# Moving v's transposes into the accumulator's PSUM tile for ten slots, one of v's copies to VectorE, and weight steps 3 to 7 up to a slot sooner

## The chip, the cores and the metric

The kernel runs on one core of a Trainium2 chip. The metric is the device time of one execution in microseconds (us), the median of several runs of the same program.

## What is computed

Attention with a sliding window, followed by a spectral mixing layer. Cut to what matters:

```python
# attention: q, k, v are [8 batches, 8 heads, 576 positions, 64]
scores = q @ k.T / sqrt(64)
rel = pos[:, None] - pos[None, :]
scores = where((rel >= 0) & (rel < 128), scores - slope[h] * abs(rel), -1e9)
x = softmax(scores) @ v                      # put together as [8, 576, 512]
# mixing: w_r, w_i are [64 modes, 512, 512] f32; w_ch is [512, 512]
X = rfft(x, axis=1)[:, :64]                  # Xr, Xi
Yr = einsum('bmd,mde->bme', Xr, w_r) - einsum('bmd,mde->bme', Xi, w_i)
Yi = einsum('bmd,mde->bme', Xr, w_i) + einsum('bmd,mde->bme', Xi, w_r)
u = x + irfft(Y, n=576, axis=1)
out = u + maximum(u @ w_ch, 0)
```

Most of the bytes are w_r and w_i, 134 MB together; q, k and v are 28 MB and the output is 9 MB.

## The kernel before

**Units, pairs and slots.** A unit is one batch and one pair of heads (128 of the 512 columns of x). Units go two by two, as pairs (two batches, same heads). There are 16 pairs: pairs 0 to 3 hold the first 128 columns of x for all eight batches (group 0), pairs 4 to 15 hold the other 384 (group 1). `_slot(g, n)` is called for n = 0 to 35 and writes out, by hand, the order of the work on every engine. Slot n works on pair d = n // 2, its first half when n is even (e = 0) and its second half when n is odd (e = 1); it prepares pair d + 1 and finishes pair d - 1. Every engine runs its own instructions in the order in which `_slot` issued them.

**What a slot does, in order.** `_score(h=0)`: the score matmuls on TensorE (L463, tile `sc`, one buffer), the exponential on ScalarE (L469), the product with the mask on VectorE (L477). In the first seven slots one more head's mask is made on ScalarE (L310). `_tr` (L413) and `_evac` (L423): a part of the next pair's q or k is transposed on TensorE into tile `tqk` (two buffers) and copied to SBUF as T; ScalarE does these copies, except four at the start. Any weight steps in the list `w0` come next. `_vnat`: v, which has been transposed once, is transposed back in 128-row pieces (L442), and VectorE copies it out (L446); this is done into the unused end of tile `av`. Then `_score(h=1)`; more `_tr`/`_evac` (in even slots two parts of q and k, in odd slots both parts of v: part 0 is 128x640, part 1 is 128x512); the casts of pair d + 2 on GpSimd (L402); one spectrum of a finished batch (L556); `_av`, the product of the probabilities with v for pair d - 1 (L494, into `av`) and its normalization on VectorE (L510, L512, and in odd slots L516); and the weight steps in the list `w1`.

**Tile `av`** has one buffer. In slot n it is written first by `_vnat` and later by `_av`; slot n + 1 may write it only when VectorE's L512 and L516 of slot n have read it. **Tile `acc`**, also one buffer, holds the weight steps' sums; it serves `_expand0` (as `xq`) and one spectrum (as `xtl`) too, all of them from slot 10 on.

**Weight steps of group 0.** `_quad(g, u)`, u = 0 to 31, multiplies four modes of w_r (u even) or w_i (u odd) with the spectra (L756, 16 matmuls). Steps 4c to 4c + 3 add up in one `acc` tile, which ScalarE copies out after the last of them (`_evac0`, L768). `_expand0` spreads the spectra of eight modes (xq L736 on TensorE, L737 and L741 on VectorE into `z0`); it runs in the slot whose `w1` begins with a step divisible by 4. The main loop hands each slot its steps: slots 10 and 11 in the call of `_slot` in the second loop, slots 12 to 31 by the tuple `share`.

**Loads.** All loads are issued by SyncE in one program order and run on the same 16 DMA engines. q, k and v of a pair are six loads of 288 KB (L375). A weight step's load is 1 MB (L654). Steps 0, 1, 4 and 5 are loaded into a ring of four places, 2 and 3 into a spare place; from step 6 on, a load of step u goes to place u % 4, whose content must have been used. `_send` runs after each slot from slot 10 on and issues the loads that the counter `g.used` allows:

```python
need = u - 3 if u >= 8 else u - 5      # group 0
if g.used < need:
    return
```

After slot 35 come the weight steps of group 1, `_pair` (L790), whose loads of 1.5 MB (L671) go through a ring of three places in the same manner; in this stage TensorE does the other half of the mixing (L837, L841, L842) beside them. `_finish` then adds up and stores the output (L824, L960, L963).

Of the kernel before, what the change touches and what calls it, by code (L numbers as in the profile page):

```python
# [9 lines left out]
FP32 = mybir.dt.float32  # L10
# [6 lines left out]
P = 128  # L17
# [16 lines left out]
def kernel(  # L34
# [16 lines left out]
    g = Ctx()  # L51
# [57 lines left out]
    with tc.manual_schedule(engines={ET.SP, ET.PE, ET.Activation, ET.DVE, ET.Pool}):  # L109
        with ExitStack() as wctx:  # L110
            wpool = wctx.enter_context(tc.tile_pool(name="wpool", bufs=1))
            A = len(GROUPS[-1])
            g.wring = wpool.tile([P, RING * 2 * A * DM], FP32)
            aux = g.wring[:, 4 * QUAD * DM :].bitcast(BF16)
            g.sel = aux[:, 0 : QUAD * P].rearrange("p (a c) -> p a c", a=QUAD)
            g.z0 = aux[:, 512:1280].rearrange("p (a i m b) -> p a i m b", a=QUAD, i=3, m=MB)
            g.own = aux[:, 1280:1344]
            g.own4 = g.wring[:, 4 * QUAD * DM + 700 : 4 * QUAD * DM + 704]
            g.used = 0
            mctx = ExitStack()  # L120
            g.mpsum = mctx.enter_context(
                tc.tile_pool(name="mpsum", bufs=1, space=bass.MemoryType.PSUM, side="right"))
            with ExitStack() as actx:
                g.work = actx.enter_context(tc.tile_pool(name="work", bufs=2))
                g.ps2 = actx.enter_context(
                    tc.tile_pool(name="ps2", bufs=1, space=bass.MemoryType.PSUM))
                g.ps1 = actx.enter_context(
                    tc.tile_pool(name="ps1", bufs=2, space=bass.MemoryType.PSUM))

                loaded = (g.first[1] + LA) // 2  # L130
                first = [(d, w) for d in range(loaded) for w in range(3)]
                first[3 * loaded - 3 : 3 * loaded - 3] = [(None, 1), (None, 4)]
                first[3 * loaded - 6 : 3 * loaded - 6] = [(None, 0)]
                first.append((None, 5))
                _begin(g, first)
                n1 = H - 1
                with tc.tile_pool(name="tmpc", bufs=1, side="right") as tp:
                    _consts(g, tp)
                    for w in range(3):
                        _cast(g, 0, w)  # L140
                    _consts2(g)
                    for w in range(2):
                        for part in range(2):
                            _tr(g, 0, w, part)
                            _evac(g, 0, w, part, nc.vector if w == 1 else None)
                    for w in range(2):
                        _cast(g, 1, w)
                    nc.scalar.activation(g.one, g.one, AF.Exp, scale=-1.0)
                    _mask(g, 0)
                    for n in range(n1):  # L150
                        _begin(g, first)
                        _slot(g, n)
                        if n == 3:
                            _select(g)
                    _begin(g, first)
                    assert not first
                start = g.first[1] + 2
                zx = ctx.enter_context(tc.tile_pool(name="zx", bufs=1, side="right"))
                g.ZTa = zx.tile([P, 4, 4, 2, 16, 8], FP32)
                spare = g.ZTa.rearrange("p e k i m b -> p (e k i m b)").rearrange("p (w r) -> p w r", w=2)  # L160
                for u in (2, 3):
                    _load_q(g, u, spare[:, u % 2])
                g.sent = 6
                for n in range(n1, start + 2):
                    if g.first[1] <= n <= start and n % 2 == 0:
                        _load(g, n // 2 + LA // 2)
                        if n == start:
                            _load(g, n // 2 + LA // 2 + 1, (0, 1))
                    _slot(g, n, [2] if n > start else [], [[0, 1], [3]][n - start] if n >= start else [])
                    if n >= start:  # L170
                        _send(g)

                share = ((), (4,)), ((5,), (6,)), ((7,), (8,)), ((), (9,)), ((10,), (11,)), ((), (12,)), \
                    ((), (13,)), ((), (14,)), ((), (15,)), ((), (16,)), ((), (17,)), ((), (18,)), \
                    ((), (19,)), ((), (20, 21)), ((22,), (23,)), ((), (24, 25)), ((26,), (27,)), \
                    ((), (28, 29)), ((), (30,)), ((), (31,))
                for n in range(start + 2, N + 2 + TAIL):
                    if n % 2 == 0:
                        _load(g, n // 2 + LA // 2, (2,))
                        _load(g, n // 2 + LA // 2 + 1, (0, 1))  # L180
                    i = n - start - 2
                    _slot(g, n, *(share[i] if i < len(share) else ()))
                    _send(g)
                    if N - 7 <= n < N - 3:
                        _load_wch(g, n - N + 7)
                    if N - 2 <= n < N + 2:
                        _cast_wch(g, n - N + 2)
            zp = ctx.enter_context(tc.tile_pool(name="zpool", bufs=1, side="right"))
            g.ZT = g.ZTa.bitcast(BF16).rearrange("p e k a m (b t) -> p e k (a m) b t", t=2)[..., 0]
            g.Z = zp.tile([P, B, DM], BF16)  # L190
            g.ZW = zp.tile([P, B, DM], BF16)
            last = len(GROUPS) - 1
            with ExitStack() as xctx:
                xt = xctx.enter_context(tc.tile_pool(name="xts", bufs=2))
                xps = xctx.enter_context(
                    tc.tile_pool(name="xps", bufs=2, space=bass.MemoryType.PSUM))
                eps = xctx.enter_context(
                    tc.tile_pool(name="eps", bufs=1, space=bass.MemoryType.PSUM))
                ftq = _ft_steps(g, xt, xps)
                g.Xz = {}  # L200
                _expand(g, 0, xt, xps)
                k, xT = 0, None
                for i in range(NM - 4):
                    m, w = divmod(i, 2)
                    m *= 2
                    _pair(g, m, w)
                    _send(g)
                    if i % MB == 5:
                        _expand(g, m // MB + 1, xt, xps)
                    if i == 2 * RING - 1:  # L210
                        xT = _xt(g, 0, xt, xps)
                    while k < len(g.seq) and k * (NM - 4 - 2 * RING) < (i + 1 - 2 * RING) * len(g.seq):
                        nxt = _xt(g, k + 1, xt, xps) if k + 1 < len(g.seq) else None
                        _xw(g, k, xT, xps)
                        xT, k = nxt, k + 1
                    if i > 2 * RING and ftq:
                        ftq.pop(0)()
                    if 0 <= i - (NM - 14) < B:
                        _z_early(g, i - (NM - 14), eps)
            g.fps = ctx.enter_context(  # L220
                tc.tile_pool(name="fps", bufs=3, space=bass.MemoryType.PSUM))
            g.mm, g.y = {}, {}
            for i in range(3):
                _known(g, i)

            wps = mctx.enter_context(
                tc.tile_pool(name="wps", bufs=1, space=bass.MemoryType.PSUM))
            g.idle = wps.tile([P, DM], FP32)
            for m in (NM - 4, NM - 2):
                for w in range(2):  # L230
                    _pair(g, m, w, BUSY)
                    _send(g)
            mctx.close()
        _finish(g)
# [73 lines left out]
def _mask(g, h):  # L308

    g.nc.scalar.activation(g.mask[:, h], g.rel, AF.Exp, scale=-(2.0 ** (-8.0 * (h + 1) / g.H)))  # L310
# [122 lines left out]
def _vnat(g, d, e, av):  # L433
# [2 lines left out]
    u = g.two[d]  # L436
    i0, n = ((0, 3), (6, 2))[e]
    c0 = (4 + e) * (g.D + 1) + e
    vt = av[:, :, c0 : c0 + n * g.D].bitcast(BF16)
    for i in range(2 * n):  # L440
        h, t = divmod(i0 + i, g.ST)
# [152 lines left out]
def _slot(g, n, w0=(), w1=()):  # L594
# [3 lines left out]
    d, e = divmod(n, 2)  # L598
# [20 lines left out]
    av = g.ps2.tile([P, 2, 512], FP32, tag="av", name="av") if here or old else None  # L619
    if here:  # L620
        _vnat(g, d, e, av)
        _score(g, d, e, 1)
# [6 lines left out]
    if e == 1 and nxt:  # L629
        for part in range(2):  # L630
            _tr(g, d + 1, 2, part)
            _evac(g, d + 1, 2, part)
    if d + 2 < N:
        for w in ((0,), (1, 2))[e]:
            _cast(g, d + 2, w)
# [361 lines left out]
```

## Time and profile before

| | before |
|---|---|
| median of 3 runs | 436.73 us (436.57 to 437.23) |
| the profiled execution's own time | 438.21 us |
| its span in the profile | 436.4 us |
| TensorE / VectorE / ScalarE / GpSimd busy | 73% / 53% / 49% / 24% |
| q, k, v and weights, read from HBM | 163.58 MB |
| mean DMA rate over the span | 398 GB/s |

The span runs from the first to the last instruction on the core. Busy shares are averages over stages with different limits: slots 0 to 35 take the first 168 us, the weight steps of group 1 follow up to about 400 us, `_finish` takes the rest. ScalarE's two exponentials per slot (L469) tell where the slots lie: slot 4 begins at 30.77 us, slot 8 at 48.44, slot 10 at 56.90, slot 11 at 63.33, slot 12 at 67.87, slot 17 at 92.92. "Granted clock" is the share of TensorE's full clock that the profile records. A wait is told as who waited and what ended the wait.

### The profile page before, as it was taken

To read this page: it belongs to the slowest core of one execution; us is meant where nothing else is said; L and a number is where in the kernel's file an instruction comes from. 1 tells how busy PE (TensorE), PEld (TensorE's weight loads), DVE (VectorE), ACT (ScalarE), POOL (GpSimd) and SP (SyncE) were. 2 spreads that over 40 slices of the span, in tenths; PEclk is the share of its full clock that TensorE was granted. 3 is DMA by queue.
4 is the path that set the end of the run, shared out by engine and by line. 5 is a ranking of instruction groups with operands and counts; after the bars stand their busy time and mean duration, and the time that the engine had idled before them with its cause. 6 is when DMAs were issued, how large, how long until landed. Compare 5 with 4: busy or idle time off the path is not lost.

```text
span 436.4 us, 11040 instructions
## 1 busy us (share of the span) xinstructions
PE 316.5 (73%) x4684; PEld 206.1 (47%) x4684; DVE 230.6 (53%) x420; ACT 215.1 (49%) x326; POOL 103.0 (24%) x160
## 2 busy tenths in 40 slices
PE   2778798878889787556766655756656588879994
PEld 1456566666667664433343333333333355535552
DVE  6466877757787674053243243332532454612884
ACT  4799978778898660122243222222222234312883
POOL 8755545433454201000000000000000000000983
PEclk9988999989999997586578688666686778969999
DMA  8999999999999999999999999999999999993787
GB/s 298 409 412 417 416 362 382 372 417 421 418 419 381 421 429 430 426 426 430 428 416 430 426 419 425 430 430 427 429 430 426 430 427 418 413 425 140 281 316 273
DMA packets 33665, 173.73 MB, mean 398 GB/s; under 512 B 3792, under 2 KB 3792, under 8 KB 21456
## 3 DMA queue, kind: packets, MB, share of 16 engines
q1 hardware_dynamic: 33616, 173.03, 96.8%
q8 instruction: 36, 0.59, 0.5%
q14 instruction: 13, 0.11, 0.1%
HBM read 163.58 MB, written 9.44 MB: 396 GB/s over the span
## 4 chain that ended last, share of the span: by engine, by line
DMA 44%; PE 26%; ACT 15%; DVE 11%; issue 3%; SPq 0%; POOL 0%; ACTq 0%; POOLq 0%
DMA wring<-in_moe_w_r_dram 23%; DMA wring<-in_moe_w_i_dram 21%; ACT att L469 7%; PE acc L790 4%; DVE att L477 3%; ACT T L423 3%; PE sc L463 2%; PE acc L756 2%; PE mm L824 2%; PE av L494 2%; PE y L824 2%; PE tqk L413 2%; DVE x_sb L512 2%; PE xw L837 2%; PE av L442 1%
## 5 line engine op out<-in xcount | busy, mean ns | idle before, releaser
L841 ACT CAST hl<-xw 64x512 bf16<-64x512 f32 x72 | 41.8, 580 | 119.6 <-PE xw L837 85.1
L790 PE MATMUL acc<-Xz,wring 128*128 128x32 bf16 x1464 | 48.8, 183 | 63.8 <-DMA wring<-in_moe_w_i_dram 35.3
L790 PEld LDWEIGHTS <-wring 128*128 128x128 bf16 x1464 | 43.4, 101 | 95.4 <-DMA wring<-in_moe_w_i_dram 50.3
L842 DVE TENSOR_TENSOR hl<-xw,hl 64x512 bf16<-64x512 f32 x72 | 49.6, 689 | 66.2 <-ACT hl L841 64.1
L963 POOL TENSOR_TENSOR o<-r,ys 128x512 f32<-128x512 f32 x18 | 22.6, 1278 | 230.9 <-DVE r L955 229.5
L469 ACT ACTIVATE att<-sc 128x1024 bf16<-128x1024 f32 x64 | 67.0, 1047 | 19.6 <-PE sc L463 19.3
L477 DVE TENSOR_TENSOR att<-att,hl 128x1024 bf16<-128x1024 bf16 x64 | 54.9, 857 | 38.8 <-ACT att L469 38.4
L423 ACT COPY T<-tqk 128x640 bf16<-128x640 bf16 x92 | 66.1, 770 | 4.5 <-PE tqk L413 4.4
L402 POOL CAST hl<-hl 128x576 bf16<-128x576 f32 x64 | 44.4, 722 | 50.2 <-issue 36.9
L837 PE MATMUL xw<-wch,xT 128*128 128x512 bf16 x144 | 53.1, 507 | 1.0 <-ACT FT L350 1.0
L413 PE MATMUL tqk<-ident_b,hl 128*128 128x128 bf16 x288 | 27.8, 237 | 9.7 <-POOL hl L402 6.4
L463 PE MATMUL sc<-T,T 64*128 64x256 bf16 (+2 forms) x320 | 26.5, 261 | 6.5 <-ACT att L469 5.2
L817 DVE COPY xT<-tp 128x512 bf16<-128x512 bf16 x36 | 15.1, 421 | 29.9 <-PE tp L815 29.6
L402 POOL CAST b<-hl 128x576 bf16<-128x576 f32 x32 | 25.3, 816 | 17.1 <-issue 10.8
L413 PEld LDWEIGHTS <-hl 128*128 128x128 bf16 x288 | 19.3, 105 | 18.9 <-issue 8.4
L837 PEld LDWEIGHTS <-xT 128*128 128x128 bf16 x144 | 17.2, 125 | 20.9 <-issue 15.7
L494 PE MATMUL av<-hl,att 128*128 128x65 bf16 (+1 forms) x576 | 24.0, 199 | 3.3 <-DVE hl L446 1.9
L587 ACT CAST Xz<-xz 128x384 bf16<-128x384 f32 x16 | 7.7, 479 | 34.8 <-PE xz L581 24.7
L442 PE MATMUL av<-ident_b,T 128*128 128x128 bf16 x160 | 15.2, 229 | 11.1 <-DVE x_sb L512 6.6
L494 PEld LDWEIGHTS <-att 128*128 128x128 bf16 (+1 forms) x576 | 20.3, 102 | 6.3 <-issue 2.3
L512 DVE TENSOR_TENSOR x_sb<-av,rec 128x512 bf16<-128x512 f32 x32 | 22.1, 691 | 1.1
L756 PE MATMUL acc<-wring 128*128 128x64 bf16 x480 | 18.7, 193 | 4.5 <-DMA wring<-in_moe_w_i_dram 1.6
(112 smaller groups left out, 454.7 us busy)
## 6 DMA issues: line engine op xcount, KB each, us to landing
wring<-in_moe_w_i_dram SPq DMA_DIRECT2D x30, 1536.0 KB, 10.1
wring<-in_moe_w_r_dram SPq DMA_DIRECT2D x30, 1536.0 KB, 10.1
wring<-in_moe_w_r_dram SPq DMA_DIRECT2D x15, 1024.0 KB, 9.1
wring<-in_moe_w_i_dram SPq DMA_DIRECT2D x15, 1024.0 KB, 9.2
hl<-in_q_dram SPq DMA_DIRECT2D x32, 288.0 KB, 6.6
hl<-in_k_dram SPq DMA_DIRECT2D x32, 288.0 KB, 6.2
hl<-in_v_dram SPq DMA_DIRECT2D x32, 288.0 KB, 7.7
out_dram<-o SPq DMA_DIRECT2D x32, 256.0 KB, 2.9
```

Of the source, the lines that this page charges most:

```text
L402: g.nc.gpsimd.tensor_copy(u.b[w][:, :, e], u.raw[w][e])
L413: g.nc.tensor.transpose(u.tp[:, r - r0], u.b[w][:, r].rearrange("p u d -> p (u d)"), g.ident_b)
L423: copy(u.T[w].rearrange("c h (p r) -> c (h p) r", r=g.R)[:, :, r0:r1], u.tp[:, 0 : r1 - r0].rearrange("c r p -> c p r"))
L463: nc.tensor.matmul(sc[:, e, c0 : c0 + nq], lhsT=kT[es, h, _start(kt) : _start(kt) + P], rhs=qT[es, h, kt * P : kt * P + nq], start=True, s ...
L469: nc.scalar.activation(a, sc, AF.Exp, scale=1.0 / math.sqrt(g.D))
L477: nc.vector.tensor_tensor(out=a, in0=a, in1=m, op=ALU.mult)
L494: nc.tensor.matmul(av[o, h, t * (D + 1) : (t + 1) * (D + 1)], lhsT=u.att[min(kt // 2, 1), h][:, f, c0 : c0 + m], rhs=vn[:, g.ST * h + kt, ...
L512: nc.vector.tensor_tensor(out=xo, in0=avv[:, :, 0:4, 0:D], in1=rec[:, :, 0:4].unsqueeze(-1).broadcast_to([P, 2, 4, D]), op=ALU.mult)
L790: nc.tensor.matmul(acc[:, et, :, m - c0 : m - c0 + 2, :], lhsT=w[:, a].bitcast(BF16)[:, 1::2][:, et * P : (et + 1) * P], rhs=X[:, a, 1 - k ...
L837: nc.tensor.matmul(xw, lhsT=xT[:, dt], rhs=g.wch[:, dt], start=(dt == 0 and g.way[n] != "q"), stop=(dt == 3))
L841: nc.scalar.copy(g.hl[hi, n, h], xw[hi])
L842: nc.vector.tensor_tensor(out=g.hl[lo, n, h], in0=xw[hi], in1=g.hl[hi, n, h], op=ALU.subtract)
```

## The change

In slots 0 to 9, `_vnat` transposes into a fresh `acc` tile (named `vt`) instead of the end of `av`. In the odd ones of these slots the copy of v's second part (128x512) goes to VectorE instead of ScalarE. Five weight steps run up to a slot sooner: 3 goes from the end of slot 11 to its middle, and 4 from the end of slot 12 to the end of slot 11; with it goes the `_expand0` of steps 4 to 7. 5 and 6 go from slot 13 to slot 12, and 7 from the middle of slot 14 to the end of slot 13. From step 8 on all is as before. `_send` is not edited, but sees `g.used` grow sooner: the load of step 8 is issued after slot 11 instead of slot 12, those of 9 and 10 after slot 12 instead of 13, that of 11 after slot 13 instead of 14. SyncE's order of loads changes accordingly. No work is added or dropped.

```diff
-                    _slot(g, n, [2] if n > start else [], [[0, 1], [3]][n - start] if n >= start else [])
+                    _slot(g, n, [2, 3] if n > start else [], [[0, 1], [4]][n - start] if n >= start else [])
...
-                share = ((), (4,)), ((5,), (6,)), ((7,), (8,)), ((), (9,)), ((10,), (11,)), ((), (12,)), \
+                share = ((5,), (6,)), ((), (7,)), ((), (8,)), ((), (9,)), ((10,), (11,)), ((), (12,)), \
...
     c0 = (4 + e) * (g.D + 1) + e
+    if 2 * d + e < g.first[1] + 2:
+        av, c0 = g.mpsum.tile([P, 2, 256], FP32, tag="acc", name="vt"), 0
     vt = av[:, :, c0 : c0 + n * g.D].bitcast(BF16)
...
         for part in range(2):
             _tr(g, d + 1, 2, part)
-            _evac(g, d + 1, 2, part)
+            _evac(g, d + 1, 2, part, g.nc.vector if part and n < g.first[1] + 2 else None)
```

Here `start` is 10 and `g.first[1]` is 8.

## The prediction

> **What bounds the kernel now.** I read the page first: the chain that ended last, and the slices of the span for DMA.
>
> ```profile
> DMA 44%; PE 26%; ACT 15%; DVE 11%; issue 3%; SPq 0%; POOL 0%; ACTq 0%; POOLq 0%
> ...
> GB/s 298 409 412 417 416 362 382 372 417 421 418 419 381 421 429 430 426 426 430 428 416 430 426 419 425 430 430 427 429 430 426 430 427 418 413 425 140 281 316 273
> ```
>
> Loads set the end: up to slice 36 the DMA engines deliver 410 to 430 GB/s, except in slices 5 to 7 and 12. The bytes do not change, so the loads end sooner only where such a hole closes; `_finish` follows them at its own pace. Table by stretch (length, busy time of PE, PEld, DVE, ACT, POOL, clock, DMA share, GB/s):
>
> ```profile
> 17.00:57.00 40.00, 31.08 (x443) 22.50 (x441) 28.15 (x51) 38.22 (x55) 23.02 (x34) 0.91 1.03 414
> ...
> 62.00:66.00 4.00, 3.36 (x75) 2.80 (x72) 2.69 (x6) 2.72 (x5) 1.95 (x4) 1.00 0.79 285
> 66.00:74.00 8.00, 6.91 (x132) 5.37 (x133) 5.80 (x12) 6.75 (x10) 3.69 (x6) 1.00 1.04 403
> 74.00:82.00 8.00, 6.45 (x127) 5.07 (x127) 6.16 (x11) 7.00 (x10) 3.47 (x5) 1.00 0.95 334
> 82.00:134.00 52.00, 44.16 (x768) 33.74 (x765) 39.24 (x70) 44.06 (x59) 23.16 (x35) 0.97 1.02 417
> 134.00:138.00 4.00, 4.00 (x84) 3.21 (x85) 2.54 (x6) 2.65 (x5) 0.66 (x2) 1.00 0.89 336
> ```
>
> Time lost against the neighbours' rate: first hole (412 - 285) x 4 / 412 = 1.2 us, second (417 - 334) x 8 / 417 = 1.6, third (421 - 336) x 4 / 421 = 0.8. SyncE's timeline shows why (start, duration, line, load):
>
> ```profile
> 57.92 1.03 SPq L375 DMA_DIRECT2D hl<-in_k_dram  x2
> 62.37 0.56 SPq L654 DMA_DIRECT2D wring<-in_moe_w_r_dram  x1
> ...
> 72.50 0.55 SPq L654 DMA_DIRECT2D wring<-in_moe_w_r_dram  x1
> ```
>
> SyncE is silent from 58.95 to 62.37: the load of step 6 waits for step 0, the end of slot 10. The k load issued at 58.63 took 5.8 us to land, so the engines ran dry at 64.4. It waits again until 72.50 with the load of step 8, which needs step 4's place (slot 12). Both are releases by TensorE in the slots' order, so the question is how much sooner these come.
>
> **What bounds slots 1 to 9.** In 17 to 57 us ScalarE is busy 38.22 of 40 us: it sets the pace there, at about 4.15 us a slot. Its gaps come from TensorE, and TensorE's from VectorE's reading of `av` (idle before an instruction in brackets):
>
> ```profile
> 50.01 0.49 PE L442 MATMUL av<-ident_b,T 128*128 128x128 bf16 x6 [1.26 <-DVE x L516]
> ...
> 50.87 1.02 ACT L469 ACTIVATE att<-sc 128x1024 bf16<-128x1024 f32 x1 [0.73 <-PE sc L463]
> ```
>
> **Part 1, `vt` in its own tile.** In slots 2 to 9 `_vnat` no longer waits for L512/L516 of the slot before. `acc` is unused until slot 10, and its only earlier reader is L446 of the slot before, long done. Of the waits removed only two reach ScalarE: 0.87 us before slot 5's first exponential (36.38) and the 0.73 above. Gain: up to 1.6 us. `_av` still waits for L512/L516, but a few matmuls later.
>
> **Part 2, the copy on VectorE.** Five 128x512 copies (slots 1, 3, 5, 7, 9) leave ScalarE. Two copies, 640 and 512 wide, start at 47.23 and the next exponential at 48.44, 1.21 us later, so one of 512 is worth about 0.58; five are 2.9 us, all where ScalarE is the bound. On VectorE the same form cost 710 ns (L423, 128x512, two instances at the start): 5 x 0.71 = 3.6 us. VectorE has 11.9 us idle in 17 to 57, but the copy lies in a chain: exponential, product (0.85), copy (0.71), `_vnat` (0.5), scores (0.4), next slot's second exponential. Walking slots 1 to 9 with these durations, the exponentials come 0.2 us sooner in slot 2, 0.8 in slot 4, 1.5 in slot 6 and 2.6 in slot 8; not more, because this chain replaces ScalarE's queue as the limit. From slot 7 VectorE itself is full: from the first product of slot 7 (45.85) to L516 of slot 9 (57.73) it works 11.9 us with 1.8 idle, and gets two more copies of 0.63 net of overlap. It starts that stretch 1.5 us sooner and ends it 1.7 sooner. Slot 10's spectra, transposes and steps 0 and 1 hang on that L516. So the end of slot 10 comes **1.7 us sooner** (bounds: 4.5, all of both parts, and -1.3, if nothing but VectorE's two extra copies counted).
>
> [...]
>
> **Part 3, the weight steps.** Their number and cost are unchanged: 16 matmuls in 0.63 us. Slot 11 now holds steps 2, 3 and 4, `_expand0` (L736 1.03 on TensorE, L737 0.69 and L741 0.58 on VectorE) and `_evac0` (0.59 on ScalarE), which `xq` must wait for, since both use `acc`. Behind that wait TensorE queues v's transposes and `_av`. With the durations of slot 12 I get step 4's end 1.2 us after step 3's old end (67.35), that is at 68.5 instead of 72.46, and slot 12 starting 1.1 us later. Slots 12 to 14 get it back: slot 12 loses the expansion (4.96 becomes 4.4, as slot 13 took), 13 and 14 have one step less each, and 14 is then like the old 12 (4.96 instead of 5.44). By slot 15 the sum is +0.1. In the data nothing is short: loads of 2 to 5 landed by 53 us.
>
> Now the loads. Step 6's goes out at 62.37 - 1.7 = 60.7, before the engines run dry at 64.4: the first hole closes. Steps 6 and 7 keep them busy until 64.4 + 2 x 2.45 = 69.3 (1 MB at 420 GB/s takes 2.45-2.5). Step 8's load goes at 68.5 - 1.7 = 66.8 instead of 72.50, with v, q and k directly behind it on SyncE; those of 9 and 10 at about 71 instead of 73.6 and 76.9. The second hole closes too. q and k of pair 11 land about when they did (their casts come 20 us later). Closed: 1.2 + 1.6 = 2.8 us; since packets run slower while few are queued, I keep 0.2 of loss.
>
> Does compute use it? In slot 16 TensorE stood still for a load:
>
> ```profile
> 91.76 0.64 PE L756 MATMUL acc<-wring 128*128 128x64 bf16 x16 [1.61 <-DMA wring<-in_moe_w_i_dram]
> 92.33 0.40 PE L463 MATMUL sc<-T,T 64*128 64x256 bf16 x6
> ...
> 94.00 0.42 PE L463 MATMUL sc<-T,T 64*128 64x256 bf16 x6 [0.72 <-ACT att L469]
> 94.36 1.03 PE L736 MATMUL xq<-hl,wring 128*128 128x128 bf16 x4
> 95.21 1.14 PE L413 MATMUL tqk<-ident_b,b 128*128 128x128 bf16 x9
> ```
>
> That load (step 11) is now issued a slot sooner and this wait goes. Slot 17 then starts 1.7 + 1.6 - 0.1 = 3.2 us sooner, and the slots keep that. The loads are 2.6 ahead, compute 3.2; the third hole, which is SyncE waiting for step 20 while the engines drain, shrinks by the difference, 0.6 at most; I count 0.5. From 180 us on loads run without a hole (426 GB/s), so the lead reaches `_finish` whole.
>
> Sum: 1.2 + 1.6 - 0.2 + 0.5 = **3.1 us**. Against the profiled execution that is 438.21 - 3.1 = 435.1, its span 433.3; that execution lies 1.5 us above the median, so the median becomes 436.73 - 3.1 = **433.6 us**.
>
> **Rivals.** A difference under 0.2% (0.9 us) cannot be told from none here.
>
> *A, the forecast*: 55%, 432.4 to 434.8.
>
> *B, TensorE's clock.* In the lines above, `tqk` x9 takes 1.14 us where it took 0.68 in slot 15: from 94 to 98 us the granted clock is 0.56, after a stretch (90.8 to 94.2) in which TensorE was busy 1.72 of 3.4 us because of the 1.61 wait. Without the wait the spell may go, and with it 0.5 + 0.5 + 0.3 us of slow matmuls and the 1.64 us for which ScalarE then waited (99.02), partly the same. Compute gains 1.1 more, and the third hole closes fully: 0.3 to 1 us on top of the forecast, 432.2. The same spells at 22.6 to 26 and 32.8 to 36.2 follow stretches with 2.0 of 3.4 us busy and may go or move. 13%. [...]
>
> *C, no gain before slot 10.* If VectorE's chain gives back all that ScalarE saves, the first hole stays, step 8's load still goes 4 us sooner, the second hole closes and the 1.6 us wait goes: 1.5 us, 435.2. For it: VectorE's full stretch from slot 7. Against it: two gaps of ScalarE vanish in any case. 15%.
>
> *D, nothing measurable*: the packets stay slow in 74 to 82 (the DMA share is 0.95 there, at only 334 GB/s) though the loads come sooner, and C holds. 5%, 436.5.
>
> *E, slower: v's copy blocks TensorE.* It lies behind the product on VectorE, and `_vnat` of the next slot, with scores, transposes and `_av` queued behind it on TensorE, waits for it. If every one of the five copies lengthened its slot by 0.71 and ScalarE's 0.58 went into waiting, slot 10 would end 3.6 us later, the first hole would be 4.8 us, the second would close: 3.6 - 1.6 = 2.0 slower, 438.7. It decides from a delay of slot 10 of over 1.6 us. Against it: in even slots the removed waits for L512/L516 (0.66 to 1.26 us) are longer than the delay. 12%.
>
> **How the numbers follow.** The forecast is A's. Eight in ten: from B's better end, 431.8, to beyond C, 436.2; D and E and a little of the rest lie outside. Faster by over 0.2%: A, B, and most of C, 80%; within 0.2%: D and C's edge, 8%; slower: E, 12%.
>
> **What would show it.** Right: in the changed profile step 0 ends near 60.6 us, the load of step 8 is issued near 67, slices 5 to 7 read over 400 GB/s, no wait for a load stands before step 11, five L423 copies of 0.71 us appear on VectorE, and L442 waits for T there instead of L516. Wrong: slot 10 ends at 62 us or later, or these slices stay below 390, or a hole of the same size opens later.

## The result: 0.5% faster, and where the time came from

The changed kernel took 435.22 us (median of 22 runs, 434.65 to 438.8); the kernel before, run beside it, 437.67 us (22 runs, 435.96 to 439.48). The ratio of their means is 0.9951, with a 95% interval of 0.9936 to 0.9966: about 2.1 us faster (1.5 to 2.8; the medians lie 2.45 us apart). The two profiled executions lie further apart: 434.88 us with a span of 433.1, against 438.21 and 436.4, that is 3.3 us.

The page of the changed kernel, chain that ended last and DMA rate in 40 slices:

```profile
DMA 58%; PE 22%; ACT 10%; DVE 6%; issue 2%; SPq 0%; ACTq 0%
...
GB/s 289 409 412 414 418 413 396 416 421 415 418 418 422 424 432 426 395 423 433 428 423 434 426 423 431 431 424 432 417 429 432 424 426 426 426 415 128 285 315 275
```

Counted from 0, slices 5 to 7, which read 362, 382 and 372 before, now read 413, 396 and 416, and slice 12 went from 381 to 422. Slice 16 fell from 426 to 395. The table by stretch (length, busy time of PE, PEld, DVE, ACT, POOL, granted clock, DMA share, GB/s):

```profile
17.00:57.00 40.00, 32.36 (x464) 23.86 (x461) 32.36 (x61) 37.17 (x51) 25.15 (x34) 0.91 1.03 413
62.00:66.00 4.00, 3.58 (x74) 2.90 (x71) 3.16 (x6) 3.49 (x6) 1.89 (x4) 1.00 1.05 432
66.00:74.00 8.00, 6.89 (x145) 5.38 (x141) 6.37 (x11) 7.47 (x11) 4.19 (x7) 1.00 1.00 386
74.00:82.00 8.00, 6.51 (x103) 4.67 (x100) 5.93 (x12) 6.95 (x10) 3.40 (x5) 1.00 1.03 426
82.00:134.00 52.00, 45.32 (x820) 34.53 (x819) 40.54 (x74) 45.35 (x61) 23.23 (x34) 1.00 1.02 418
134.00:138.00 4.00, 2.33 (x39) 1.78 (x40) 1.61 (x3) 2.70 (x5) 1.78 (x3) 1.00 1.00 418
```

All three holes are closed (285, 334 and 336 before; 432, 426 and 418 now), and the clock is full from 82 to 134 us. Of these stretches only 66 to 74 reads lower than before: (412 - 386) x 8 / 412 = 0.5 us lost there. But a new hole opens behind them, in slice 16 (before, then now):

```profile
174.00:182.00 8.00, 4.44 (x123) 3.56 (x121) 0.72 (x2) 0.96 (x2) 1.44 (x10) 0.50 1.01 426
```

```profile
174.00:182.00 8.00, 4.48 (x124) 3.65 (x121) 0.00 (x0) 0.26 (x1) 0.00 (x0) 0.50 0.96 383
```

That is (426 - 383) x 8 / 426 = 0.8 us. When the same kernel was profiled again (the first run below), it read 423 GB/s there, so this hole belongs to the one execution. SyncE's timeline shows the releases (start, duration, line, load; the line numbers behind `_vnat` are two higher than before):

```profile
58.06 1.05 SPq L375 DMA_DIRECT2D hl<-in_k_dram  x2
60.28 0.56 SPq L656 DMA_DIRECT2D wring<-in_moe_w_r_dram  x1
60.93 0.55 SPq L656 DMA_DIRECT2D wring<-in_moe_w_i_dram  x1
66.29 0.54 SPq L656 DMA_DIRECT2D wring<-in_moe_w_r_dram  x1
```

Step 6's load leaves at 60.28 instead of 62.37, step 8's at 66.29 instead of 72.50. And step 11 in TensorE's timeline starts 4.64 us sooner, with no wait in brackets:

```profile
87.12 0.63 PE L758 MATMUL acc<-wring 128*128 128x64 bf16 x16
```

In the chain of waits the last weight load ends at 398.47 before (start and duration, one line of each kernel):

```profile
388.86 9.61 DMA wring<-in_moe_w_i_dram
```

and at 395.18 now:

```profile
385.62 9.56 DMA wring<-in_moe_w_i_dram
```

3.3 us sooner, which is the whole difference of the spans. In the experiments' profiles too the span ended 37.8 to 38.1 us after the last weight load had landed, so the end follows this landing.

### The profile page after: what moved, and what is told of

It is laid out like the page before. It is cut to its first block, busy times and chain, and to the rows that moved or that the text cites. A ratio compares the mean times of both kernels' runs of the same rounds, so it can differ in the third digit from the quotient of the medians.

```text
span 433.1 us, 11017 instructions
## 1 busy us (share of the span) xinstructions
PE 317.3 (73%) x4684; PEld 206.2 (48%) x4684; DVE 232.8 (54%) x425; ACT 212.4 (49%) x321; POOL 104.3 (24%) x160
## 4 chain that ended last, share of the span: by engine, by line
DMA 58%; PE 22%; ACT 10%; DVE 6%; issue 2%; SPq 0%; ACTq 0%
DMA wring<-in_moe_w_r_dram 30%; DMA wring<-in_moe_w_i_dram 19%; PE acc L792 4%; ACT att L471 4%; DMA hl<-in_k_dram 3%; DMA hl<-in_q_dram 3%; PE mm L826 2%; DMA ZTa<-in_moe_w_r_dram 2%; PE av L496 2%; PE acc L758 2%; PE y L826 2%; PE xw L839 2%; ACT T L423 2%; DVE att L479 2%; DVE hl L844 1%
## 5 line engine op out<-in xcount | busy, mean ns | idle before, releaser
L792 PEld LDWEIGHTS <-wring 128*128 128x128 bf16 x1464 | 43.3, 101 | 94.8 <-DMA wring<-in_moe_w_i_dram 51.3
L423 ACT COPY T<-tqk 128x512 bf16<-128x512 bf16 (+1 forms) x87 | 62.2, 758 | 4.2 <-PE tqk L413 3.6
L402 POOL CAST hl<-hl 128x576 bf16<-128x576 f32 x64 | 46.1, 748 | 45.2 <-issue 33.4
L839 PE MATMUL xw<-wch,xT 128*128 128x512 bf16 x144 | 55.2, 524 | 0.7 <-ACT FT L350 0.7
L758 PEld LDWEIGHTS <-wring 128*128 128x128 bf16 x480 | 16.3, 99 | 6.0 <-DMA wring<-in_moe_w_r_dram 2.6
```

Of the source, the lines that this page charges most:

```text
L402: g.nc.gpsimd.tensor_copy(u.b[w][:, :, e], u.raw[w][e])
L423: copy(u.T[w].rearrange("c h (p r) -> c (h p) r", r=g.R)[:, :, r0:r1], u.tp[:, 0 : r1 - r0].rearrange("c r p -> c p r"))
L758: nc.tensor.matmul(acc[:, et, :, h : h + QUAD, :], lhsT=w[:, a].bitcast(BF16)[:, 1::2][:, et * P : (et + 1) * P], rhs=g.z0[:, a, 1 - k : 3 ...
L792: nc.tensor.matmul(acc[:, et, :, m - c0 : m - c0 + 2, :], lhsT=w[:, a].bitcast(BF16)[:, 1::2][:, et * P : (et + 1) * P], rhs=X[:, a, 1 - k ...
L839: nc.tensor.matmul(xw, lhsT=xT[:, dt], rhs=g.wch[:, dt], start=(dt == 0 and g.way[n] != "q"), stop=(dt == 3))
```

## The experiments

Part 1 is `vt` in the `acc` tile, part 2 the five copies of v on VectorE, part 3 the weight steps (with the sooner loads that follow from them). Diffs are against the changed kernel, except the last, which is against the kernel with the old lists of steps. Ratios are against the kernel before, with 95% intervals; the other columns come from one profiled execution each.

| kernel | median us (runs) | ratio | span us | step 0 starts | step 8's load |
|---|---|---|---|---|---|
| whole change, run again | 435.68 (6) | 0.9939 (0.9922 to 0.9956) | 433.6 | 59.32 | |
| parts 1 and 2 | 436.75 (12) | 0.9973 (0.9954 to 0.9991) | 435.0 | 59.02 | 69.80 |
| parts 1 and 2, again | 436.03 (12) | 0.9968 (0.9949 to 0.9987) | 433.6 | 59.82 | |
| part 3 alone | 436.17 (12) | 0.9960 (0.9944 to 0.9977) | 434.4 | 60.69 | 67.37 |
| all, loads of 8 to 11 held back | 435.34 (6) | 0.9932 (0.9915 to 0.9950) | 433.1 | 59.60 | 68.05 |
| part 1 alone | 435.86 (5) | 0.9955 (0.9933 to 0.9977) | 433.4 | 59.20 | 69.98 |
| part 1 alone, again | 435.85 (12) | 0.9966 (0.9949 to 0.9984) | 433.4 | 59.48 | |
| part 2 alone | 440.24 (6) | 1.0052 (1.0025 to 1.0080) | 439.1 | 64.70 | |
| parts 1 and 3 | 435.31 (12) | 0.9942 (0.9924 to 0.9960) | 433.6 | 59.48 | |
| parts 1 and 2, step 11 a slot later | 436.19 (8) | 0.9954 (0.9938 to 0.9970) | 433.4 | 59.60 | |
| before, step 11 a slot later | 437.11 (12) | 0.9990 (0.9970 to 1.0011) | 435.4 | 61.25 | |
| before, second profile | 437.98 (1) | | 436.2 | 60.70 | |

**The whole change once more**, no edit:

> The whole change again, as the yardstick for the kernels run beside it. Both theories: ratio 0.995 (0.9935 to 0.9965), about 2.1 us faster; step 0 starts near 59.6 us, no hole over 0.3 us in the loads between 58 and 66 us and 0.5 us lost between 66 and 72 us.

435.68 us, ratio 0.9939. It repeats, and serves as the mark for the kernels run beside it.

**Parts 1 and 2 without part 3**: the old lists of steps.

```
-  _slot(g, n, [2, 3] if n > start else [], [[0, 1], [4]][n - start] if n >= start else [])
+  _slot(g, n, [2] if n > start else [], [[0, 1], [3]][n - start] if n >= start else [])
...
-  share = ((5,), (6,)), ((), (7,)), ((), (8,)), ((), (9,)), ((10,), (11,)), ((), (12,)), \
+  share = ((), (4,)), ((5,), (6,)), ((7,), (8,)), ((), (9,)), ((10,), (11,)), ((), (12,)), \
```

> Parts 1 and 2 alone (v's transposes in their own tile for ten slots, five copies on VectorE); the weight steps stay where they were. Theory (an earlier end of slot 10 moves every later load, so it closes both holes): step 0 starts near 59.6 us, step 6's load goes at 60.3, step 8's at 70.4 instead of 72.5, while the engines stay busy to 73.7; the second hole shrinks from 1.6 to 0.5 us and step 11's wait of 1.6 us mostly goes; 2.3 us faster or nearly what the whole change gives. Rival (each part closes one hole, the gains add): only the first hole closes, 1.2 us faster, and 74 to 82 us stays near 334 GB/s.

Its table by stretch, columns as above:

```profile
62.00:66.00 4.00, 3.33 (x66) 2.60 (x63) 3.15 (x6) 3.76 (x6) 2.06 (x3) 1.00 1.05 421
66.00:74.00 8.00, 6.51 (x130) 5.24 (x129) 6.52 (x12) 6.94 (x10) 4.60 (x6) 1.00 1.03 402
74.00:82.00 8.00, 6.59 (x113) 4.94 (x110) 5.59 (x10) 6.46 (x9) 2.73 (x5) 1.00 1.00 408
82.00:134.00 52.00, 44.24 (x762) 33.94 (x760) 38.18 (x70) 42.22 (x56) 22.45 (x32) 0.93 1.01 412
134.00:138.00 4.00, 4.00 (x84) 3.28 (x83) 2.52 (x6) 3.85 (x6) 1.62 (x2) 1.00 0.84 303
```

Both early holes all but closed without part 3, and yet the gain was 1.2 us (0.27%). The last but one line and the last tell why in this execution: at step 11 TensorE waited longer than before,

```profile
89.80 0.64 PE L758 MATMUL acc<-wring 128*128 128x64 bf16 x16 [2.35 <-DMA wring<-in_moe_w_i_dram]
```

then ran at half clock from 90.3 to 97.2, and step 20 came at 132.66, only 1.26 us sooner than before (133.92). So the third hole grew to (421 - 303) x 4 / 421 = 1.1 us. The loads were ahead, the slots not.

**Part 3 alone**: parts 1 and 2 taken out.

```
-    if 2 * d + e < g.first[1] + 2:
-        av, c0 = g.mpsum.tile([P, 2, 256], FP32, tag="acc", name="vt"), 0
...
-            _evac(g, d + 1, 2, part, g.nc.vector if part and n < g.first[1] + 2 else None)
+            _evac(g, d + 1, 2, part)
```

> Part 3 alone (weight steps 3 to 7 sooner, and their loads with them); slots 0 to 9 as before. Theory: step 0 starts at 61.7 us as before, the first hole stays (62 to 66 us near 285 GB/s), step 8's load goes near 68.5 us, the second hole closes (74 to 82 us over 415 GB/s), step 11 does not wait: 1.5 us faster. Rival (without the earlier slots the crowded slot 11 costs what the loads gain): no difference, slot 12 and all after it 1 us later.

```profile
62.00:66.00 4.00, 3.62 (x71) 2.91 (x68) 2.24 (x5) 3.18 (x5) 1.28 (x2) 1.00 0.95 370
66.00:74.00 8.00, 6.84 (x141) 5.36 (x138) 6.49 (x13) 7.47 (x10) 4.09 (x7) 1.00 0.94 363
74.00:82.00 8.00, 6.60 (x116) 4.89 (x117) 5.75 (x12) 6.95 (x11) 3.90 (x6) 1.00 1.03 426
...
134.00:138.00 4.00, 2.17 (x45) 1.70 (x42) 1.91 (x4) 2.99 (x5) 2.42 (x4) 1.00 1.00 421
```

Nearly the mirror image: the first hole does not close but spreads (370 GB/s in 62 to 66 us, (412 - 370) x 4 / 412 = 0.4 us lost, and 363 in 66 to 74, another 1.0), the second and third close, step 11 (88.21) has no wait and step 20 comes at 129.45. 1.7 us (0.40%), near the 1.5 that rival C had for this.

**Do the sooner loads do it, or the sooner steps?** The whole change, with the loads of steps 8 to 11 held back by a slot or so:

```
-            need = u - 3 if u >= 8 else u - 5
+            need = {8: 6, 9: 8, 10: 8, 11: 9}.get(u, u - 3) if u >= 8 else u - 5
```

> The whole change, but the loads of steps 8 to 11 are held back to the slots after which they went before the change (needs of 6, 8, 8 and 9 used steps instead of 5, 6, 7 and 8), so SyncE's order of loads is that of before. Theory (part 3 acts through the loads): step 8's load goes near 70 us instead of 66.3, as in the kernel with parts 1 and 2 alone, and the time is that kernel's, 0.3 to 0.8 us slower than the whole change. Rival (part 3 acts through TensorE's order, the loads were early enough): same as the whole change within 0.2 us.

No change in time (0.9932 beside 0.9939), although step 8's load left 1.76 us later than in the whole change (not the 3.7 expected):

```profile
68.05 0.55 SPq L656 DMA_DIRECT2D wring<-in_moe_w_r_dram  x1
```

Step 11, at 88.05, waited 0.77 us for its load, and no spell of slow clock followed. 66 to 74 us reads 412 GB/s here instead of 386, so the 0.5 us lost there was not decisive either. My theory fell: the loads were soon enough without their sooner release. That part 3 works through the place of the steps in TensorE's order is what is left, but it is not shown. TensorE came to step 11 at 87.28 us here (88.05 - 0.77) and at 87.45 with parts 1 and 2 alone (89.80 - 2.35), almost the same; the waits differ because the load landed 1.75 us sooner here.

**Part 1 alone**, the old lists of steps (as above) and:

```
-            _evac(g, d + 1, 2, part, g.nc.vector if part and n < g.first[1] + 2 else None)
+            _evac(g, d + 1, 2, part)
```

> Part 1 alone: v's transposes in their own tile in slots 0 to 9; no copy moves, the weight steps stay. Walk of the prediction: only the two gaps of ScalarE that end with scores queued behind a wait for L516 go (0.87 and 0.73 us), step 0 starts 0.7 to 1.6 us sooner (60.1 to 61.0 us). Rival (the waits are only moved to the product with v at the slot's end): 61.5 to 61.8 us. The time follows the compute lead at step 20: 0 to 1 us faster.

0.9955, and run again 0.9966. That is already most of the gain. ScalarE's load is unrelieved (busy 39.29 of 40 us from 17 to 57 us, 37.17 in the whole change), but step 0 comes no later. The profiles of all kernels here, grouped by what they do in slots 0 to 9, say why (starts in us; the normalization is the last of slot 9 on VectorE, on which slot 10 hangs, L516, in the changed kernels L518):

| slots 0 to 9 | normalization | slot 10 on ScalarE | step 0 |
|---|---|---|---|
| as before (4 profiles) | 56.42 to 57.45 | 55.88 to 56.90 | 60.69 to 61.71 |
| part 1, without the copies (3) | 54.94 to 55.22 | 54.39 to 54.67 | 59.20 to 59.48 |
| parts 1 and 2 (6) | 54.75 to 55.50 | 53.56 to 54.31 | 59.02 to 59.82 |

With the copies ScalarE begins slot 10 about 0.5 us sooner, but VectorE's normalization and step 0 come no sooner than without them. Part 1 alone brings all of it: 1.7 us, by the means behind the first two rows.

**Part 2 alone**: the old lists of steps (as above), and `vt` back in `av`.

```
-    if 2 * d + e < g.first[1] + 2:
-        av, c0 = g.mpsum.tile([P, 2, 256], FP32, tag="acc", name="vt"), 0
```

> Part 2 alone: the five copies of v on VectorE; v's transposes stay in the tile of the product, and wait for L516 of the slot before, which now comes 0.6 us later in odd slots. If part 2 needs part 1: step 0 starts at 61.2 us or later, less than 0.5 us sooner, and the waits of L442 for L516 grow to 1.5 to 2 us. Rival (ScalarE's saving counts by itself): step 0 starts near 60 us.

0.5% slower. In TensorE's timeline (idle before the instruction in brackets):

```profile
32.59 0.79 PE L442 MATMUL av<-ident_b,T 128*128 128x128 bf16 x6 [1.81 <-DVE x L516]
...
42.41 0.51 PE L442 MATMUL av<-ident_b,T 128*128 128x128 bf16 x6 [1.18 <-DVE x L516]
...
51.40 0.51 PE L442 MATMUL av<-ident_b,T 128*128 128x128 bf16 x6 [1.78 <-DVE x L516]
```

The copies delay L516, and with `vt` still in `av` every second `_vnat` stands behind it, for 1.81, 1.18 and 1.78 us where before it stood for 1.26, 0.66 and 1.26. A half-clock spell (53.1 to 60.0) follows the last of them, step 0 comes at 64.70, 3 us later than in the first profile of before, and 62 to 66 us falls to 233 GB/s. How much of this is the waits' and how much the spell's is not separated. This is close to rival E, made real by taking away part 1; only that `_vnat` waits here for L516, which the copies delay, and not for the copy itself.

**Parts 1 and 3, without part 2**: the `_evac` edit of part 1 alone, on the new lists.

> Parts 1 and 3, without the copies on VectorE. If part 2 is worth nothing once part 1 is there (step 0 started at 59.2 us with part 1 alone and at 59.0 with parts 1 and 2): step 0 starts at 59.2 us, the time is that of the whole change within 0.2%, ratio 0.994 to 0.995. Rival (part 2 pays where ScalarE is the bound): step 0 a microsecond later than in the whole change, near 60.5, and 0.3% slower than it.

0.9942 beside the whole change's 0.9939. Part 2 brings nothing that can be measured here. This is the simpler version and not a faster one.

**Part 1 alone again, and parts 1 and 2 again**, to weigh part 2 once more with more runs:

> Part 1 alone, a second time, beside parts 1 and 2 on the same chip. Theory (the times differ by whether TensorE's clock halves after the wait for step 11): the profile shows no half clock between 85 and 100 us and the ratio is 0.995 to 0.996 again, or it shows one and the ratio is near 0.997. Rival (part 2 costs by itself): 0.2% faster than parts 1 and 2 whatever the clock does.

> Parts 1 and 2 alone, a second time. Theory: ratio near 0.997 together with a half clock after the wait for step 11 near 90 us and under 330 GB/s in 134 to 138 us; without that spell the profiled execution is 1.5 us shorter in its span than the first one (435.0), like part 1 alone. Rival: the same span near 435 us with no such spell.

0.9966 and 0.9968: no difference. Part 1 alone, which was expected at 0.995 to 0.996 without a half clock at step 11, came out a little above that: there was none there (a wait of 0.92 us, clock 1.00 from 86 to 98 us), but one at 128.4 to 131.8. The second profile of parts 1 and 2 has a shorter wait and no slow clock near 90 us (one at 58.1 to 61.5 instead):

```profile
89.68 0.64 PE L758 MATMUL acc<-wring 128*128 128x64 bf16 x16 [0.82 <-DMA wring<-in_moe_w_i_dram]
```

```profile
134.00:138.00 4.00, 2.95 (x58) 2.40 (x57) 2.21 (x6) 3.74 (x6) 2.61 (x4) 1.00 1.01 412
```

Its third hole is almost gone and its span is 433.6 instead of 435.0. So the same kernel with and without the spell behind step 11 differs by 1.4 us, one execution each, though step 0 was 0.8 us later in the faster one and its three stretches from 62 to 82 us read lower (393, 386 and 384 GB/s).

**Is it step 11's wait?** Parts 1 and 2 with step 11 a slot later (it goes from the end of slot 16 to the middle of slot 17, and step 10 from the middle of slot 16 to its end):

```
-  share = ((), (4,)), ((5,), (6,)), ((7,), (8,)), ((), (9,)), ((10,), (11,)), ((), (12,)), \
+  share = ((), (4,)), ((5,), (6,)), ((7,), (8,)), ((), (9,)), ((), (10,)), ((11,), (12,)), \
```

> Parts 1 and 2, and of part 3 nothing; instead step 11 goes from the middle of the pair at the end of slot 16 to the middle of slot 17, so that TensorE reaches it after its load has landed (89.8 us in the kernel with parts 1 and 2 alone, where it waited 2.35 us and the clock was halved for 6.8 us). Theory (the gain is the smaller of the loads' lead and the slots' lead at step 20, and the wait with the half clock behind it took the slots' lead): no wait for a load at step 11, no half clock between 85 and 100 us, step 20 starts at 130.5 us or sooner, 134 to 138 us over 400 GB/s, ratio 0.994 to 0.995 like the whole change. Rival (steps 3 to 7 themselves had to come sooner): like parts 1 and 2 alone, ratio 0.997.

0.9954. Step 11 at 89.57 waits 0.42 us, no slow clock follows, step 20 comes at 129.56 (132.66 without the edit), and the third hole is gone:

```profile
134.00:138.00 4.00, 2.46 (x44) 1.80 (x41) 2.11 (x4) 3.24 (x6) 2.29 (x3) 1.00 1.00 420
```

The span is 433.4, as in the whole change, with steps 3 to 10 not moved sooner at all. In the times the step is within the intervals (0.9973 and 0.9968 without the edit), so this rests on the profile.

**The same single move in the kernel before** (the edit just shown, without parts 1 and 2), and the kernel before profiled again:

> The kernel before with one step moved: 11 goes from slot 16 to the middle of slot 17, nothing else. Theory (the time is set by the loads' holes; the slots' lead at step 20 decides the third): holes one and two stay, TensorE does not stand still at step 11 and keeps its clock, step 20 starts 1.5 us or more sooner than 133.9 us, 134 to 138 us goes from 336 to over 400 GB/s, 0.8 us faster. Rival (the third hole follows from the first two, whose lost time moves the loads): no difference.

> The kernel before, once more, for its profile. If the half clock follows the wait for step 11 by chance of where the clock's windows fall: a spell of another length (none, 3.4 or 6.8 us) starting between 88 and 98 us, and the longer it is, the lower the rate in 134 to 138 us and the longer the span. Rival: the same spell of 3.4 us from 94 us and 336 GB/s in 134 to 138 us.

The move alone gives 0.9990, with an interval (0.9970 to 1.0011) that holds both no change and the 0.8 us expected: not resolved. Its profile shows the mechanism: no stand before step 11, and

```profile
134.00:138.00 4.00, 3.03 (x62) 2.38 (x60) 2.67 (x5) 2.64 (x4) 1.74 (x2) 1.00 1.02 421
```

with a span of 435.4 beside 436.4 and 436.2. The second profile of before has the wait again (1.89 us) and again 3.4 us of slow clock behind it (93.3 to 96.7), and 317 GB/s in the third hole. Its spells of slow clock in the early slots lie elsewhere (one at 21.6 to 28.5, none at 32.8 to 36.2). Its step 0 starts at 60.70, a microsecond sooner than in the first profile (61.71), and its first hole is small (399 GB/s).

## Why the prediction was right, and which of its terms were not

**Direction and range held, and the mechanism in the main.** The holes that were to close did, by the releases that were named. Step 0 ended at 60.25 us (forecast 60.6), step 8's load left at 66.29 (66.8), slot 12 began at 66.62 (67.3), the first two holes closed, step 11's wait went, and its last named sign held too: `_vnat` waits for T now and no longer for L516 (TensorE's timeline of the changed kernel):

```profile
31.81 0.51 PE L444 MATMUL vt<-ident_b,T 128*128 128x128 bf16 x6 [0.77 <-DVE T L423]
```

For the profiled pair the sum was 3.1 and the span shrank by 3.3, but that they meet so closely is partly luck. Two of the terms were off in opposite directions: 0.5 instead of 0.2 was lost between 66 and 74 us, and the third hole closed fully, 0.8 instead of 0.5. (For the 0.2 the prediction said that packets run slower while few are queued. In its table the two holes read 285 GB/s at a DMA share of 0.79 and 334 at 0.95, that is 361 and 352 per whole share, against 417 at 1.02, or 409, from 82 to 134 us.) And the lead did not reach `_finish` whole: the hole at 174 to 182 us took 0.8. About as much came back in stretches that the sum does not list: the closed first and second hole read above their neighbours' rate (432 and 426), 138 to 142 us reads 424 instead of 393, and 198 to 298 us 428 instead of 426.

**The size over many runs is smaller**: 2.1 us (1.5 to 2.8). The median of 435.22 lies above the 432.4 to 434.8 given to A and on rival C's 435.2. It is not C's mechanism, since the first hole closed. Of the 1.6 us to the forecast of 433.6, 0.9 is the kernel before, at 437.67 over 22 runs instead of 436.73 over three, and the rest is gain that did not come. The forecast took its terms from one profile of before, and the second one shows that they vary: the first hole was 1.2 us there and (412 - 399) x 4 / 412 = 0.1 us here, the second 1.6 there and (417 - 351) x 8 / 417 = 1.3 here. The spell of slow clock at 32.8 to 36.2 us stands in the one with the larger first hole and the later slot 10, and not in the other; that it is the reason is likely but not shown.

**The mis-sized term is part 2.** The prediction counted 2.9 us of ScalarE's time for the five copies and let VectorE's chain give part of it back. The copies do cost what it said (VectorE's groups by form, 17 to 57 us):

```profile
L423 DVE COPY T<-tqk 128x512 bf16<-128x512 bf16 x5 | 3.6, 715 | 0.0
```

but with and without them the times agree: 0.9939 and 0.9942 with part 3, 0.9968 and 0.9966 without it; in the first pair, 0.9973 and 0.9955, the intervals overlap. The step that failed is the one that made slot 10's gain a sum of both parts. Slot 10 hangs on VectorE's last normalization of slot 9, and that starts at 54.75 to 55.50 us with the copies and at 54.94 to 55.22 without. So the 1.7 us of slot 10 came as forecast, but all of it from part 1, which the prediction had at up to 1.6; part 2 adds nothing to it.

**A mechanism like rival E's exists, but part 1 takes it away.** The argument against it, that the removed waits are longer than the delay, holds only as long as part 1 removes them. Alone, the same copies cost 0.5%.

**Part 3's working was right in its result, and its cause is open.** It gained what was said, but not through the sooner release of the loads of steps 8 to 11: held back, they changed nothing. In all its profiles, with and without parts 1 and 2, step 11 waits 0.77 us or not at all, no slow clock follows, and step 20 is soon enough to close the third hole. Whether the steps' order in TensorE does this was not tried by itself.

**The parts do not add.** Part 1 alone saves 0.34 to 0.45%, part 3 alone 0.40%, both 0.49 to 0.61%. The difference is about as large as the intervals. The prediction's rule for the third hole, that what the loads have gained there must be matched by the slots, would explain it, and the first profile of parts 1 and 2 follows it: the early holes closed and the gain was lost at step 20; with step 11 moved the same kernel kept it. In the second profile the third hole nearly closed, and the early ones stayed in part. Rival B was therefore half right. The spell at 94 us went, the third hole closed, but the time stayed above its 432.2, since the third hole of that profile had no more than 0.8 us to give, 0.3 over what the forecast took.

**What stays open.** The spells of slow clock come and go between executions of the same kernel; the two profiles of parts 1 and 2 suggest what one costs, but no run set them at will. How part 3 keeps step 11 from waiting is open, and so is what held the loads at 174 to 182 us. The effect of step 11's place in the kernel before is not resolved by its times. And why the DMA engines, busy all the time, deliver only 386 GB/s between 66 and 74 us was not tried.

## What to carry to other kernels

Find the holes in the queue that bounds the kernel, name the instruction that releases each, and count a saving on any engine only as far as it brings that instruction forward: 2.9 us off the busiest engine were worth nothing measurable here, because the release hung on the engine that got the work. Time each part of a change alone and in pairs: one part here is harmful alone and worth nothing beside another, and two good ones together seem to give less than their sum. Where a queue runs ahead, look for the next hole: of the queue's lead no more is kept than the releasing engine has gained by then.

## What the runs showed of the hardware that was not expected

TensorE's clock sometimes halved behind stretches in which it was not idle but half busy. In the kernel before (1.72 us busy of 3.4, clock still 1.00, then 0.50 from 94.2 us):

```profile
90.80:94.20 3.40, 1.72 (x35) 1.47 (x36) 1.04 (x4) 1.85 (x4) 1.02 (x2) 1.00 1.01 419
```

In these profiles waits of 1.61 to 2.35 us before step 11 were followed by 3.4 or 6.9 us of slow clock, and waits of 0.42 to 0.92 us were not. Nor was the 1.36 us of part 2 alone, though TensorE was busy still less around it, with the clock at 1.00 here and after:

```profile
93.20:96.60 3.40, 1.52 (x30) 1.28 (x31) 1.46 (x3) 2.11 (x4) 0.75 (x3) 1.00 1.01 419
```

And in the second profile of part 1 alone the clock halved at 128.4 us, behind 3.4 us in which TensorE was busy 2.49. So a long wait may be paid twice, but neither its length nor the busy time alone tells when. The clock by stretch, before and with parts 1 and 2:

```profile
86.00:98.00 12.00, 9.67 (x163) 7.59 (x157) 7.32 (x14) 8.72 (x12) 4.46 (x7) 0.86 1.02 418
```

```profile
86.00:98.00 12.00, 9.51 (x129) 7.37 (x127) 6.41 (x13) 7.00 (x11) 4.30 (x6) 0.72 1.02 418
```

The slow spells keep to a step of 3.41 us in the traces of the kernel before and of the changed kernel: each begins a whole number of such steps after the one before it (before: at 22.55, 32.79 and 94.23 us, 3 and 18 steps apart), and each but the last, with which the trace ends, is a whole number of them long.

The DMA engines' busy share also hides rate: 386 GB/s at a share of 1.00 between 66 and 74 us, and 426 at 1.03 in the next stretch of the same kernel. A shallow hole is therefore read from the rate.
